# A planner for the attention part, and slot inputs by groups of four tiles, in a fused block-sparse attention and soft mixture-of-experts kernel

## The chip, the cores and the metric

The kernel runs on one core of a Trainium2 chip. The metric is the device time of one execution in microseconds. PE is the matrix engine, DVE the vector engine, ACT the scalar engine, POOL the general engine, SP the engine whose queue issues the DMAs. PE multiplies into PSUM, which has eight banks of 2 KB a partition; the other operands lie in SBUF.

## The reference

```python
# B, H, S, D = 4, 8, 768, 64; blocks of 32 rows, 24 of them
scores = scale * q @ k^T                      # scale = 1/8
mask   = |block_i - block_j| <= 1, or block_i or block_j is 0 or 23,
         or block_j is one of three sampled for block_i
attn   = softmax over the unmasked scores
x      = (attn @ v)  ->  [3072, 512]          # the eight heads side by side
# soft mixture of experts: 8 experts, 4 slots each, hidden size 1024
logits = x @ phi                              # [3072, 32]
d      = softmax(logits, over the 3072 rows)
slot_input = d^T @ x                          # [32, 512]
slot_out   = per expert: relu(slot_input @ w1) @ w2
c      = softmax(logits, over the 32 slots)
out    = c @ slot_out                         # [3072, 512], all float32
```

## The kernel before

**Attention.** Each batch has two dense query blocks (0 and 23) and 22 sparse ones, taken as 11 pairs. A pair's scores are over 256 keys for each query block: three neighbours, the two outer blocks, three sampled ones. `stage_k` puts these keys side by side in one of four buffers `kst`: POOL copies the fixed part (L214), ACT the three sampled blocks (L218), whose block numbers are loaded into registers. `stage_v` lets POOL copy the sampled V blocks into `vrs` (L229). PE multiplies queries and keys into `s` (L303) or, for the dense blocks, into `sd` (L292). DVE reduces the maximum (`nm`), ACT takes the exponential into `p`, DVE transposes it in 32 x 32 blocks into `ptt` or `ptd`, and PE multiplies with V (L375) into a product tile `avt`. `av_out` divides on DVE by the row sums and writes `x`. Eight heads are two halves `r` of four; `av_half` is one half's product for one tile. A tile `x` is 128 rows: two pairs of 64 rows, or the first pair with the dense blocks. There are six tiles in a batch.

**Slot inputs.** `moe_front` runs for each of the 24 tiles in seven steps e1 to e5: turn x (`mxt`, `xT`), logits in four parts (L487), add the parts by a product with `sel4` (L494, L495), top (`nmx`), exponential (`dT`), turn it (L517), copy `d`, sum of x weighted by d (L534), and add to `sacc` and `ssum` after scaling what was summed by `al`. Its small results lie in unused columns of `avt`.

**PSUM.** Three score banks (`SB`), two product sets of two banks, one bank for turned tiles.

**Order.** PE's and DVE's instructions stand in the order in which the loop over units writes them. `ORDER` says how dense and sparse units alternate, the lists `EOFF` after how many units each step of `moe_front` follows. Each unit is one half: a sparse unit with `r == 0` computes the scores of the whole pair. ACT, POOL and SP are ordered by the scheduler of the language.

**Weights.** 64 weight tiles of 512 KB. `NPRE` of them are loaded during attention, three into a K buffer and six into V's first buffer late in it, three more into the other K buffer; the rest comes into space that attention has released (`lwb`, V's second buffer) and into freed tiles. After attention come the experts' two layers and the combination, with the output stores.

Of the kernel before, what the change touches and what calls it, by code (L numbers as in the profile page):

```python
# [21 lines left out]
P = 128  # L22
# [13 lines left out]
NKST, NVR, NQ = 4, 6, 3  # L36
PB, PTB, XB = 4, 3, 2
SB = 3

ORDER0 = "DDSSDDSS"  # L40
ORDER = "DSSDDDSS"
KSTEP, VSTEP, EARLY = 5, 1, 4
KEARLY = 4


EOFF = [(3, 2), (5, 1), (5, 2), (6, 0), (7, 2), (7, 2), (8, 1)]
EOFFL = [(3, 1), (4, 1), (4, 2), (5, 0), (5, 1), (5, 1), (5, 2)]
# [8 lines left out]
NPRE, NLB = 12, 11  # L56
KW = {"ktile": 3, "v0": 6, "v1": 6}
W0, W1 = 3, 3
# [3 lines left out]
MAN = {mybir.EngineType.PE, mybir.EngineType.DVE}  # L62
TMAN = MAN | {mybir.EngineType.Activation}


@with_exitstack
def attn_moe_kernel(ctx, tc, qT, kT, vtab, sampled, phi, w1, w2, out):
# [49 lines left out]
    sacc = const.tile([P, P], F32, name="sacc")  # L117
# [50 lines left out]
    qd = pst.tile([P, NP, 2, BLK], F32, name="qd")  # L168
    qc = [pst.tile([P, NP, 2, BLK], F32, name=f"qc{n}") for n in range(NQ)]


    avt = psA.tile([P, 2, 2, 512], F32, name="avt", tag="av", bufs=1)
    def load_k(b):
        ktile[b] = pk.tile([P, NP, S], F32, name="ktile", tag="ktile")
        SP.dma_start(out=qd, in_=qT[b, 0])
        for p in range(NP):
            SP.dma_start(out=ktile[b][:, p, :], in_=kT[b, p])

    def load_v(b):
        vb = vbuf[b % 2].rearrange("p (a f) -> p a f", a=2)  # L180
        if b < 2:
            for p in range(NP):
                (DVE if b == 0 and p < 2 else POOL).memset(vb[32 * p:32 * p + 32, 1 - p % 2, :], 0.0)  # L183
        for p in range(NP):
            SP.dma_start(out=vb[32 * p:32 * p + 32, p % 2, :], in_=vtab[b, 32 * p:32 * p + 32, :])
        vtile[b] = vb.rearrange("p a (k r d) -> p a k r d", k=NBZ, r=2)


    def load_q(b, g):
        SP.dma_start(out=qc[(b * NG2 + g) % NQ], in_=qT[b, g + 1])  # L190

# [10 lines left out]
    def stage_k(b, i):  # L202
        n = nsp[0] % NKST
        nsp[0] += 1
        st = kst[n]
        kv = ktile[b]
        if kfresh.get(n) != b:
            kfresh[n] = b
            POOL.tensor_scalar(out=st[:, :, 128:192].rearrange("p c (g s) -> p c g s", g=2),
                               in0=kv.rearrange("p c (g s) -> p c g s", g=NB)[:, :, 0:NB:NB - 1, :],  # L210
                               scalar1=SCALE, scalar2=1.0, op0=ALU.mult, op1=ALU.mult)

        w, r0 = (0, 96) if i % 2 else (32, 0)
        POOL.tensor_scalar(out=st[:, :, w:w + 96], in0=kv[:, :, (i - 1) * BLK:(i + 2) * BLK],  # L214
                           scalar1=SCALE, scalar2=1.0, op0=ALU.mult, op1=ALU.mult)
        vals = block_numbers(sreg, i, mybir.EngineType.Activation, NB - 1)
        for j, o in enumerate((r0, 192, 224)):
            ACT.activation(out=st[:, :, o:o + BLK],  # L218
                           in_=kv[:, :, ds(vals[j] * BLK, BLK)], func=AF.Copy, scale=SCALE)
# [771 lines left out]
```

## Time and profile before

| what | value |
|---|---|
| median of 3 runs | 456.62 us (454.41 to 459.93) |
| the profiled execution | 454.29 us, its span 452.5 us, mean clock 0.885 |
| busy in the span | PE 351.7, DVE 248.1, ACT 183.9, POOL 170.5 us |
| DMA | 60.30 MB, mean 133 GB/s |

A row of a timeline is start, length, engine, line, operation, result<-operands, shape, count, and in brackets the idle time before it with what ended it. A fp32 matmul of the program is two records in the trace. A row of a stretch is its start and end, its length, busy us of PE, PEld (weight load), DVE, ACT and POOL with the number of instructions, PE's granted clock as a share of full, busy share of the DMA, and GB/s. A group's row ends in busy us, mean ns | idle time ahead of it and what ended it. A row of waits is the total in us, how often, the longest.

### The profile page before, as it was taken

Reading aid. Unit: us, or ns where it says so; the run is one execution under the profiler, and the core shown is the slowest. Engines: PE = TensorE matmul, PEld = TensorE weight load, DVE = VectorE, ACT = ScalarE, POOL = GpSimd, SP = SyncE. Lnnn points to the kernel's source line nnn. Section 1 sums busy time; section 2 is a strip of 40 time slices with the busy share of each in tenths; the row PEclk is TensorE's granted clock in tenths of the full one; section 3 lists DMA queues with packets and bytes.
Section 4 is the critical chain, followed back from the end, with each engine's and each line's share of the span. In section 5 each row is a group of like instructions: output and inputs, shape, how many; then the busy total and the mean of one; then the engine's idle time right before and its main releaser. Section 6 shows DMA issues by size and latency. Waiting matters only on the chain.

```text
span 452.5 us, 17984 instructions
## 1 busy us (share of the span) xinstructions
PE 351.7 (78%) x7381; PEld 230.7 (51%) x7381; DVE 248.1 (55%) x611; ACT 183.9 (41%) x628; POOL 170.5 (38%) x397
## 2 busy tenths in 40 slices
PE   5686977787979777878988778779786588899860
PEld 1145645454666555554855555547564356435440
DVE  7673646666556655766285558573855762401240
ACT  1544445544255545533374446252652421301340
POOL 7597145464122555633034465330433331300000
PEclk9998879899789988899698889897986887999896
DMA  8439492414310005052010043500000406999998
GB/s 237 102 114 217 169 369 91 133 47 99 76 27 28 28 13 165 27 114 63 14 38 14 25 154 116 191 25 14 26 27 1 143 1 199 403 409 406 410 335 258
DMA packets 26083, 60.30 MB, mean 133 GB/s; under 512 B 2833, under 2 KB 15250, under 8 KB 25490
## 3 DMA queue, kind: packets, MB, share of 16 engines
q1 hardware_dynamic: 26002, 59.16, 40.3%
q8 instruction: 58, 0.95, 0.9%
q14 instruction: 23, 0.19, 0.1%
HBM read 52.86 MB, written 6.29 MB: 131 GB/s over the span
## 4 chain that ended last, share of the span: by engine, by line
PE 50%; DVE 27%; DMA 11%; issue 4%; ACT 4%; ACTq 1%; DVEq 0%; SPq 0%
PE avt L375 34%; DMA w<-in_w_dram 9%; PE s L303 6%; DVE ptt L342 4%; DVE nm L319 4%; DVE x L371 4%; PE sd L292 2%; DMA kw<-in_w_dram 2%; DVE nm L310 2%; PE avt L487 2%; PE mlt L494 2%; DVE xT L329 2%; ACT p L322 2%; DVE v L183 1%; DVE rs L370 1%
## 5 line engine op out<-in xcount | busy, mean ns | idle before, releaser
L229 POOL COPY vrs<-v 128x260 f32 x264 | 96.4, 404 | 83.1 <-PE avt L375 69.7
L375 PE MATMUL avt<-v,ptt 64*64 64x130 f32 (+2 forms) x1728 | 95.2, 326 | 27.4 <-DVE sacc L539 23.1
L319 DVE TENSOR_REDUCE nm<-s 128x2 f32<-128x512 f32 x88 | 58.2, 663 | 63.2 <-PE s L303 62.9
L375 PEld LDWEIGHTS avt<-v,ptt 64*64 64x64 f32 (+2 forms) x1728 | 62.7, 150 | 55.4 <-DVE sacc L539 27.1
L218 ACT ACTIVATE kst<-ktile 128x128 f32 x264 | 63.6, 304 | 62.2 <-PE s L303 47.9
L322 ACT ACTIVATE p<-s,nm 128x256 f32<-128x256 f32 x176 | 71.9, 468 | 30.0 <-DVE nm L319 28.5
L214 POOL TENSOR_SCALAR kst<-ktile 128x384 f32<-128x384 f32 x88 | 44.1, 512 | 102.8 <-PE s L303 102.7
L303 PE MATMUL s<-kst,qc 64*32 64x256 f32 x1408 | 57.1, 400 | 6.7 <-ACT p L322 4.1
L342 DVE STREAM_TRANSPOSE ptt<-p 128x512 f32<-128x512 f32 x88 | 61.5, 698 | 0.2 <-ACT p L322 0.2
L375 PE MATMUL avt<-vrs,ptt 64*32 64x130 f32 x2112 | 56.7, 312 | 0.0
L375 PEld LDWEIGHTS avt<-vrs,ptt 64*32 64x32 f32 x2112 | 45.8, 121 | 0.4
L292 PE MATMUL sd<-ktile,qd 64*32 64x384 f32 x256 | 32.2, 584 | 16.6 <-ACT pd L316 9.8
L303 PEld LDWEIGHTS s<-kst,qc 64*32 64x32 f32 x1408 | 26.7, 110 | 23.5 <-issue 10.4
L369 DVE TENSOR_SCALAR rs<-avt 128x8 f32<-128x8 f32 (+3 forms) x33 | 5.4, 163 | 59.0 <-PE avt L375 27.0
L375 PE MATMUL avt<-v,ptd 64*64 64x130 f32 x768 | 32.4, 342 | 5.2 <-issue 3.9
L316 ACT ACTIVATE pd<-sd,nb 128x384 f32<-128x384 f32 x32 | 16.8, 576 | 45.1 <-DVE nb L313 32.6
L375 PEld LDWEIGHTS avt<-v,ptd 64*64 64x64 f32 x768 | 31.2, 177 | 6.3 <-issue 4.2
L327 ACT COPY lp<-avt 128x128 f32<-128x128 f32 x23 | 6.1, 265 | 50.1 <-issue 30.3
L292 PEld LDWEIGHTS sd<-ktile,qd 64*32 64x32 f32 x256 | 9.5, 116 | 31.9 <-ACT pd L316 14.5
L310 DVE TENSOR_REDUCE nm<-sd 128x1 f32<-128x384 f32 x32 | 16.8, 543 | 8.8 <-PE sd L292 8.5
L371 DVE TENSOR_TENSOR x<-avt,rs 128x512 f32<-128x512 f32 (+3 forms) x33 | 20.1, 609 | 1.1
L534 PE MATMUL avt<-x,d 128*32 128x128 f32 x192 | 10.8, 300 | 11.7 <-DVE d L329 11.7
(107 smaller groups left out, 354.9 us busy)
## 6 DMA issues: line engine op xcount, KB each, us to landing
w<-in_w_dram SPq DMA_DIRECT2D x34, 512.0 KB, 9.7
v<-in_w_dram SPq DMA_DIRECT2D x18, 512.0 KB, 6.3
v<-in_vtab_dram SPq DMA_DIRECT2D x16, 406.2 KB, 7.3
ktile<-in_kT_dram SPq DMA_DIRECT2D x16, 384.0 KB, 5.2
kw<-in_w_dram SPq DMA_DIRECT2D x12, 512.0 KB, 8.9
qc<-in_qT_dram SPq DMA_DIRECT2D x44, 128.0 KB, 2.1
out_dram<-ob SPq DMA_DIRECT2D x20, 256.0 KB, 4.3
qd<-in_qT_dram SPq DMA_DIRECT2D x4, 128.0 KB, 2.2
```

What stands on the lines that cost most here:

```text
L214: POOL.tensor_scalar(out=st[:, :, w:w + 96], in0=kv[:, :, (i - 1) * BLK:(i + 2) * BLK], scalar1=SCALE, scalar2=1.0, op0=ALU.mult, op1=ALU. ...
L218: ACT.activation(out=st[:, :, o:o + BLK], in_=kv[:, :, ds(vals[j] * BLK, BLK)], func=AF.Copy, scale=SCALE)
L229: POOL.tensor_copy(out=st[:, :, j:j + 1, :], in_=vf[:, :, ds(vals[j], 1), :])
L292: PE.matmul(u.s[n][32 * p:32 * p + 32, :], lhsT=qd[s_, p, u.j, :], rhs=kt[s_, p, 384 * n:384 * (n + 1)], start=True, stop=True)
L303: PE.matmul(u.pair_of[r].s[32 * p:32 * p + 32, j, :], lhsT=q[s_, p, j, :], rhs=kst_[s_, p, :], start=True, stop=True)
L310: DVE.tensor_reduce(out=nm[:, n:n + 1], in_=u.s[n], axis=AX.X, op=ALU.max, negate=True)
L316: ACT.activation(out=u.p[n], in_=u.s[n], func=AF.Exp, bias=nb, scale=SCALE)
L319: DVE.tensor_reduce(out=nm, in_=u.s, axis=AX.X, op=ALU.max, negate=True)
L322: ACT.activation(out=u.p[:, hf, :], in_=u.s[:, hf, :], func=AF.Exp, bias=nm[:, hf:hf + 1], scale=1.0)
L342: DVE.transpose(out=u.pt[:, :, n:n + 2, :].rearrange("p k j q -> p j k q"), in_=u.p.rearrange("p j (k q) -> p j k q", k=8))
L371: DVE.tensor_tensor(out=x, in0=a[:, :, :, 0:D], in1=rs[lo:hi].unsqueeze(3).to_broadcast([hi - lo, 2, 2 * n, D]), op=ALU.mult)
L375: PE.matmul(av[o:o + m, g, r * 2 * D1:(r + 1) * 2 * D1].rearrange("p (a d) -> p a d", a=2), lhsT=lhsT, rhs=rhs, start=start, stop=stop)
```

## The change

The whole of the attention and slot-input part is described as tasks with engine, estimated duration, dependencies, a key, and the buffers that they take. `Plan.run` takes the tasks one after the other, always the one that can start first by its estimates (then the one with the lower key), and so sets the order of all five engines. Some tasks may go to one of two engines.

```diff
-NKST, NVR, NQ = 4, 6, 3
-PB, PTB, XB = 4, 3, 2
-SB = 3
-ORDER0 = "DDSSDDSS"
-ORDER = "DSSDDDSS"
+NKST, NVR, NQ = 4, 6, 4
+PB, PTB, XB, XTB = 4, 4, 6, 4
+SB, MB = 4, 2
-NPRE, NLB = 12, 11
+NPRE, NLB = 7, 11
-MAN = {mybir.EngineType.PE, mybir.EngineType.DVE}
+MAN = {E_.PE, E_.DVE, E_.Activation, E_.Pool, E_.SP}
+LAG = {"PE": 0.25, "DVE": 0.18, "ACT": 0.22, "POOL": 0.17, "SP": 0.0}
+    def run(self):
...
+            for t in avail:
...
+                if ok:
+                    for e, d in t.opts:
+                        c = (max(r, at[e]), t.key, max(r, at[e]) + d)
+                        if best is None or c < best[0]:
+                            best = (c, t, e, d)
...
+            if e == "SP":
+                dma = max(dma, st + 1.4) + t.byte / 0.4e6
+                t.fin = dma + 0.3
...
+    plan = Plan(dict(s=SB, av=1, pt=MB, p=PB, ptt=PTB, kst=NKST, vrs=NVR, x=XB, xT=XTB, k=2, v=2, q=NQ,
+                     ptd=1, lp=1, dT=1, d=1), free=("pt",))
...
-    avt = psA.tile([P, 2, 2, 512], F32, name="avt", tag="av", bufs=1)
+        T.av = psA.tile([P, 2, 512], F32, name="av", tag="av", bufs=1)
...
-            for p in range(NP):
-                (DVE if b == 0 and p < 2 else POOL).memset(vb[32 * p:32 * p + 32, 1 - p % 2, :], 0.0)
+                for a in range(2):
+                    SP.dma_start(out=vb[:, a, lo:hi], in_=vfull[b, :, a * VH + lo:a * VH + hi])
...
-            POOL.tensor_scalar(out=st[:, :, w:w + 96], in0=kv[:, :, (i - 1) * BLK:(i + 2) * BLK],
-                               scalar1=SCALE, scalar2=1.0, op0=ALU.mult, op1=ALU.mult)
+            POOL.tensor_copy(out=st[:, :, w:w + 96], in_=kv[:, :, (i - 1) * BLK:(i + 2) * BLK])
...
+        r = add(sampled_, [("ACT", 0.62), ("POOL", 0.73)], [f, t_sreg], n - 2.5,
+                pre=lambda e: block_numbers(sreg, i, e, NB - 1))
...
+        t_q = add(scale, [("POOL", 0.37), ("ACT", 0.37)], [t_q], n - 4.5)
...
+        t_qk = add(qk, ("PE", 1.1), [t_q] + [k for _, k in kd], n, acq=[("s", s_use[0]), ("s", s_use[1])])
...
+            t_0 = add(lambda t: heads(t, 0), ("PE", 2.2), deps, n + 0.5, acq=[("av", use)])
+            t_a = add(lambda t: heads(t, 1), ("PE", 2.2), [t_0], n + 0.5)
+            T.out = [add(lambda t: av_out(T, T.av, 0, P), ("DVE", 1.0), [t_a], n + 0.6, acq=[("x", x_use)])]
...
+            for k in range(2):
+                for p in range(NP):
+                    for r in range(2):
+                        s_ = slice(64 * r, 64 * r + 64)
+                        PE.matmul(u.s[r][k][32 * p:32 * p + 32, :], lhsT=T.dq.q[s_, p, j, :],
+                                  rhs=kt[s_, p, 384 * k:384 * (k + 1)], start=True, stop=True)
...
+        t_qk = add(qk, ("PE", 1.5), [T.dq.t, t_k[b]], n, acq=[("s", s_use[0])] * 2 + [("s", s_use[1])] * 2)
...
+            t_a = add(dense, ("PE", 5.4), T.dturned + [t_v[b]], n + 0.5, acq=[("av", use)])
...
+    def plan_group(gi, Ts, last, final=False):
...
+            t_o = add(out, [("DVE", 0.62), ("ACT", 0.5)], [t_t], n + 2.1, acq=[("xT", x_use)])
...
+            for c in range(4):
+                for j, (_, T) in enumerate(Ts):
+                    PE.matmul(st.l[32 * j:32 * j + 32, :], lhsT=phis[:, c, :], rhs=T.xT[:, c, :],
+                              start=(c == 0), stop=(c == 3))
...
+            for j, (_, T) in enumerate(Ts):
+                PE.matmul(st.ms[32 * j:32 * j + 32, :], lhsT=st.d[:, 32 * j:32 * j + 32], rhs=T.x,
+                          start=True, stop=True)
...
+            for o, i in ((sacc, st.ms), (ssum, st.sm)):
+                if gi:
+                    DVE.scalar_tensor_tensor(out=o, in0=o, scalar=st.al, in1=i, op0=ALU.mult, op1=ALU.add)
```

In `plan_group` each of four tiles has 32 of the 128 partitions, with a top and sums of its own; `sacc` is now 128 x 512 and holds four sums, one for each place in the group. At the end the four are brought to a common top (`f_row` to `f_slots`: a turn, a small reduction, an exponential, a product with `ident`, a scaled `sel4`) and added by a product. The scale 1/8 is now applied to the queries. PSUM holds four score banks, one product set of two banks and two banks for everything else. Both halves of a dense block are multiplied together.

Where the order of instructions moves, first SP at the start of the program. `scr` is for the block numbers, `qd` and `qc` are queries of before, `q` of now, `phis` is phi. Before:

```order
L129 DMA scr<-in_sampled_dram 1x144
L609 DMA qd<-in_qT_dram 128x256
L611 DMA ktile<-in_kT_dram 128x768 x4
L190 DMA qc_105<-in_qT_dram 128x256
L185 DMA v_67<-in_vtab_dram 32x3250 x4
L190 DMA qc_106<-in_qT_dram 128x256
L615 DMA phis<-in_phi_dram 128x128
```

Now:

```order
L213 DMA scr<-in_sampled_dram 1x144
L261 DMA ktile<-in_kT_dram 128x768 x4
L272 DMA v_67<-in_vfull_dram 128x910 x6
L272 DMA v_67<-in_vfull_dram 128x520 x2
L255 DMA q<-in_qT_dram 128x256 x4
L864 DMA phis<-in_phi_dram 128x128
```

The first queries have moved behind K and V, and V is twice as large, in rows of 128 partitions.

PE between the products of two tiles in the middle of batch 1; `avt` and `av` are products, `dT`, `d` and `mxt` belong to the slot inputs. Before:

```order
L303 MATMUL s<-kst_100,qc_106 32x256 x8
L303 MATMUL s<-kst_101,qc_106 32x256 x8
L517 MATMUL avt<-ident,dT 128x32
L442 MATMUL mxt<-ident,x 128x128 x4
L534 MATMUL avt<-x,d 32x128 x4
L375 MATMUL avt<-v_68,ptt 128x130 x4
L375 MATMUL avt<-v_68,ptt 64x130 x8
```

Now:

```order
L426 MATMUL s<-kst_102,q 32x256 x8
L426 MATMUL s<-kst_103,q 32x256 x8
L426 MATMUL s<-kst_100,q 32x256 x8
L426 MATMUL s<-kst_101,q 32x256 x8
L667 MATMUL mxt<-ident,x 128x128 x4
L504 MATMUL av<-v_68,ptt 128x130 x4
L504 MATMUL av<-v_68,ptt 64x130 x8
```

Two pairs of scores and a turned tile stand there now, and the two slot-input steps that waited for other engines have gone. Before, the second of the two pairs stood between the two half products of a tile.

DVE from one tile's x on, also in batch 1. Before:

```order
L369 TENSOR_SCALAR rs<-avt 128x8
L370 RECIPROCAL rs<-rs 128x8
L371 TENSOR_TENSOR x<-avt,rs 128x512
L342 STREAM_TRANSPOSE ptt<-p 128x2x8x32
L319 TENSOR_REDUCE nm<-s 128x2
L329 COPY d<-avt 128x32
L523 SCALAR_TENSOR_TENSOR ssum<-ssum,al,sm 128x1
L329 COPY xT<-mxt 128x512
```

Now:

```order
L498 TENSOR_SCALAR rs<-av 128x8
L499 RECIPROCAL rs<-rs 128x8
L500 TENSOR_TENSOR x<-av,rs 128x512
L453 STREAM_TRANSPOSE ptt<-p 128x2x8x32 x2
L441 TENSOR_REDUCE nm<-s 128x2
L294 COPY xT<-mxt 128x512
L441 TENSOR_REDUCE nm<-s 128x2 x3
```

The slot-input steps have left the place between x and the next reductions, and a tile's two transposes stand together.

More of the change, by code (lines that the diff above doesn't have):

```diff
@@ new lines, in attn_moe_kernel, with tile_of, plan_pair, qk @@
+    tiles = {}
+    def tile_of(b, t):
+        if (b, t) not in tiles:
+            T = Rec()
+            T.b, T.t, T.turned, T.staged, T.units, T.use, T.x_use = b, t, [], [], [], [], []
+            tiles[b, t] = T
+        return tiles[b, t]
+    def plan_pair(b, g, n):
+        T = tile_of(b, (g + 1) // 2)
+        w = 1 if g and g % 2 == 0 else 0
+        u = Rec()
+        u.g = g
+        kd, ku = [], []
+        for r in range(2):
+            use = []
+            kd.append(stage_k(b, 2 * g + 1 + r, n, use))
+            ku.append(use)
+        t_q, q_use = plan_q(u, b, g + 1, n)
+        s_use = [[], []]
+        def qk(t):
+            u.s = [psA.tile([P, 2, 256], F32, tag="s", name="s", bufs=SB) for _ in range(2)]
+            for j in range(2):
@@ L360, in av_out, with new_x @@
+        u.vst = []
+        for r in range(2):
+            use = []
+            v, t_s = stage_v(b, 2 * g + 1 + r, n, use)
+            u.vst.append(v)
+            T.staged.append(t_s)
+            T.use.append(use)
+        T.units.append(u)
+        if g == 0 or w:
+            plan_av(T, n)
+    def new_x(T):
+        if not hasattr(T, "x"):
+            T.x = pw.tile([P, DM], F32, tag="x", name="x", bufs=XB)
+        return T.x
+    def av_out(T, av, lo, hi, rs_=slice(0, 2), xlo=None):
         n = rs_.stop - rs_.start
@@ new lines, in f_exp, with f_col, f_sel @@
+    def f_exp(t):
+        ACT.activation(out=fin.row, in_=fin.row, func=AF.Exp)
+    def f_col(t):
+        fin.pc = bank("mc")
+        PE.matmul(fin.pc[:, 0, 0:1], lhsT=fin.row, rhs=ident[0:1, 0:1], start=True, stop=True)
+    def f_sel(t):
+        fin.w = pw.tile([P, 1], F32, tag="w1", name="w1", bufs=1)
+        DVE.tensor_copy(out=fin.w, in_=fin.pc[:, 0, 0:1])
+        fin.sel = pw.tile([P, P], F32, tag="lp", name="selw", bufs=1)
+        DVE.tensor_scalar(out=fin.sel, in0=sel4, scalar1=fin.w, scalar2=None, op0=ALU.mult)
@@ new lines, in f_sum, with f_inv, f_slots @@
+    def f_sum(t):
+        fin.ps = bank("msum")
+        PE.matmul(fin.ps[:, 0, 0:1], lhsT=fin.sel, rhs=ssum, start=True, stop=True)
+    def f_inv(t):
+        fin.tot = pw.tile([P, 1], F32, tag="tot", name="tot", bufs=1)
+        DVE.tensor_scalar(out=fin.tot, in0=fin.ps[:, 0, 0:1], scalar1=EPS, scalar2=None, op0=ALU.add)
+        DVE.reciprocal(out=fin.tot, in_=fin.tot)
+    def f_slots(t):
+        fin.sS = bank("psS")
+        for c in range(4):
+            PE.matmul(fin.sS[:, c, 0:NS], lhsT=sacc[:, c * P:(c + 1) * P], rhs=fin.sel[:, 0:NS], start=True, stop=True)
@@ L695, in attn_moe_kernel @@
[L695 to L707 removed]
+    plan.run()
     ms.__exit__(None, None, None)
@@ L711, in attn_moe_kernel @@
     ms.__enter__()
[L712 to L750 removed]
+    ssum = fin.tot
     att.close()
```

968 lines of the change are left out of this document (533 added, 435 removed).

## The prediction

> **What bounds the kernel now.** I read the totals of the page first, then its slices, to see which stages there are.
>
> ```profile
> span 452.5 us, 17984 instructions
> PE 351.7 (78%) x7381; PEld 230.7 (51%) x7381; DVE 248.1 (55%) x611; ACT 183.9 (41%) x628; POOL 170.5 (38%) x397
> ...
> PE   5686977787979777878988778779786588899860
> ...
> PEclk9998879899789988899698889897986887999896
> DMA  8439492414310005052010043500000406999998
> ```
>
> No engine is full. One slice is 11.3 us: attention reaches to about slice 33 (PE at seven or eight tenths, DMA mostly idle), then come seven slices with the DMA full. They need separate sums. Next the chain and PE's waits:
>
> ```profile
> PE 50%; DVE 27%; DMA 11%; issue 4%; ACT 4%; ACTq 1%; DVEq 0%; SPq 0%
> ...
> PE avt L375 <- DVE sacc L539: 23.1, 12, 2.8
> PE avt L534 <- DVE d L329: 11.7, 16, 2.0
> ```
>
> The chain alternates between PE and DVE, and PE's two longest waits are for `sacc` and `d`, both of the per-tile slot-input chain. One tile, PE and then DVE, shows how:
>
> ```profile
> 239.45 2.93 PE L375 MATMUL avt<-v,ptt 64*128 64x130 f32 x40 [1.81 <-DVE sacc L539]
> ...
> 243.18 0.43 PE L487 MATMUL avt<-xT,phis 128*32 128x128 f32 x8
> 243.54 1.09 PE L303 MATMUL s<-kst,qc 64*32 64x256 f32 x32
> 244.56 0.49 PE L494 MATMUL mlt<-lp,sel 128*128 128x128 f32 x2
> ...
> 245.12 1.71 PE L375 MATMUL avt<-v,ptt 64*128 64x130 f32 x40
> ...
> 247.45 1.09 PE L303 MATMUL s<-kst,qc 64*32 64x256 f32 x31
> 249.04 0.21 PE L517 MATMUL avt<-ident,dT 32*128 32x32 f32 x1 [0.50 <-ACT kst L218]
> 249.19 0.66 PE L442 MATMUL mxt<-ident,x 128*128 128x128 f32 x4
> ...
> 252.49 0.38 PE L375 MATMUL avt<-v,ptt 64*128 64x130 f32 x2 [1.82 <-DVE sacc L539]
> ...
> 244.72 0.69 DVE L319 TENSOR_REDUCE nm<-s 128x2 f32<-128x512 f32 x1 [4.71 <-PE s L303]
> ...
> 248.21 0.69 DVE L371 TENSOR_TENSOR x<-avt,rs 128x512 f32<-128x512 f32 x1
> ...
> 252.11 0.32 DVE L539 SCALAR_TENSOR_TENSOR sacc<-sacc,al,avt 128x128 f32<-128x128 f32 x1
> ```
>
> DVE waits 4.71 us for scores while PE multiplies; later DVE works without a pause and PE waits for it. They take turns, and a tile takes 13.04 us from product to product. The stretches:
>
> ```profile
> 213.50:302.00 88.50, 72.18 (x1718) 51.27 (x1718) 53.15 (x129) 41.59 (x148) 35.96 (x92) 0.88 0.22 73
> 239.45:252.49 13.04, 10.32 (x266) 7.44 (x266) 7.46 (x18) 6.73 (x26) 5.92 (x17) 0.88 0.08 23
> 151.67:163.38 11.71, 8.94 (x266) 6.32 (x266) 7.52 (x18) 6.73 (x26) 6.61 (x17) 1.00 0.09 25
> 372.00:374.00 2.00, 2.00 (x30) 1.43 (x33) 1.64 (x6) 0.00 (x0) 1.77 (x6) 0.56 0.10 16
> ```
>
> The columns are the stretch, then busy time of PE, PEld, DVE, ACT and POOL, the clock, and DMA. A batch takes 88.50 us, of which PE is idle 16.3. The same tile at clock 1.00 takes 11.71 us: PE's pauses cost 1.3 us more through the lower clock that follows them. The first half product of the tile above took 3.73 us (239.45 to 243.18), the second, without a pause, 2.33 (245.12 to 247.45).
>
> **The change, PE's work.** The planner's PE order is known, so I price it at full-clock pitches, start to start. Further rows:
>
> ```profile
> 206.10 1.49 PE L292 MATMUL sd<-ktile,qd 64*32 64x384 f32 x16
> 207.53 1.34 PE L375 MATMUL avt<-v,ptt 64*64 64x130 f32 x18
> ...
> 209.58 0.43 PE L487 MATMUL avt<-xT,phis 128*32 128x128 f32 x8
> ...
> 36.02 3.11 PE L375 MATMUL avt<-v,ptd 64*64 64x130 f32 x99 [0.40 <-DVE x L371]
> 43.06 5.25 PE L375 MATMUL avt<-v,ptd 64*64 64x130 f32 x93 [3.94 <-issue]
> ```
>
> - 44 score pairs at 1.02 us (243.54 to 244.56): 44.9.
> - 8 dense score blocks, now both row halves interleaved. A pair, interleaved already, takes 1.02 us for 32 x 256 columns; by that rate 32 x 384 take 1.53: 12.2. Bounds: 1.43 each (the second half wholly beside the first, 206.10 to 207.53) and 2.86 (no overlap), so 11.4 to 22.9. I take 12.2, the nearer kind of row. Today it is 16 x 1.43 = 22.9.
> - 40 half products at 2.33: 93.2. Four first-pair products with both halves interleaved: one half takes 2.05 (207.53 to 209.58), so between 2.05 and 4.1; I take 2.4 since the halves use different columns of the array: 9.6.
> - 4 dense products: 99 of 192 records took 3.11, so 6.0 each: 24.0.
> - 24 turned tiles at 0.66: 15.8. Logits and sums: the columns stay the same, four rounds of 0.43 per group of four tiles, 12 x 1.7 = 20.6. Twelve small transposes at 0.21: 2.5. The products with `sel4` (0.56 a tile) are gone.
>
> Sum: 222.8 us of PE work, 55.7 a batch, against 72.2 busy now.
>
> **The change, the other engines.** Per tile DVE loses `d`, `ssum`, `sacc`, the top and mostly `xT` (the order puts 20 of 24 on ACT). What stays is eight instructions of at most 0.69 us and x with two short steps, 6.6 of the 7.46 at most. ACT gives up 27 of 88 sampled K copies and three quarters of the small copies and takes xT: I leave it at its 6.73. POOL takes those 27 and 20 of the 48 query scalings, the order says. Two rows, the one of `vrs` with least, median and largest ns:
>
> ```profile
> L229 POOL COPY vrs<-v x264: 394/403/535, 28.0 to 372.5; 128x260 f32 x132
> ...
> L322 ACT ACTIVATE p<-s,nm 128x256 f32<-128x256 f32 x176 | 71.9, 468 | 30.0 <-DVE nm L319 28.5 <-DVE d L329 0.7 <-DVE rs L369 0.2
> ```
>
> At 0.4 us or less an instruction that adds about 1.5 us a tile to the 5.92 to 6.61 of now: some 7.7. PE's tile is 2 x 2.33 + 2 x 1.02 + 0.66 + a quarter group (1.0) = 8.4. So PE becomes the longest, POOL stands close behind.
>
> What stays as PE's pauses. With one product set the next tile's product waits until DVE has written x: in the tile above that is at 248.90, 1.45 us after PE went on to the next scores (247.45). Two score pairs and a turn stand between the products in the new order, 2.7 us of work: that is the cover. It holds only while the four score banks are free in time, that is while eight exponentials (0.47 us mean or less) end within the 4.7 us of two half products. I leave 0.6 us a tile for what slips (12), 4 us a batch in the dense part, where one block takes all four banks and the next scores must wait for its exponentials (16), and 4 for fetch pauses such as the 3.94 us above. 32 in all; bounds 12 (half the tile's slip, nothing else) and 75 (today's 16.3 a batch plus lost clock). With it a batch takes 63.7 us.
>
> **The start.** V of batches 0 and 1 now comes with its zeros, 3.33 MB instead of 1.66 with memsets, and the queries stand behind it in SP's queue.
>
> ```profile
> 5.36 3.53 PE L292 MATMUL sd<-ktile,qd 64*32 64x384 f32 x6 [5.36 <-DMA ktile<-in_kT_dram]
> ...
> 4.00:8.00 4.00, 2.64 (x5) 0.53 (x6) 3.24 (x3) 0.00 (x0) 2.98 (x2) 1.00 1.04 381
> 12.00:16.00 4.00, 1.21 (x2) 0.00 (x0) 2.08 (x6) 1.40 (x7) 3.96 (x4) 1.00 0.97 199
> ...
> 7.37 0.35 SPq L615 DMA_DIRECT2D phis<-in_phi_dram  x1
> ...
> phis<-in_phi_dram SPq DMA_DIRECT2D x1, 64.0 KB, 10.9
> ```
>
> K rows over 128 partitions moved at 381 GB/s, V rows over 32 partitions at 199. `phis`, issued behind V at 7.37, landed 10.9 us later, with V: what stands behind V waits for it. The new V spans 128 partitions, so 1.57 + 3.33 + 0.13 MB at 381 from 3 us on: 16.2, with the scaling 17.5 us until the first scores (5.36 today). At 199 for V it would be 25. I take 17.5 because width decides between the two rows.
>
> **The end.** From the last product on the DMA sets the pace.
>
> ```profile
> 380.48 1.67 PE L375 MATMUL avt<-vrs,ptt 64*32 64x130 f32 x46
> ...
> 372.00:382.15 10.15, 8.75 (x189) 6.57 (x189) 2.93 (x12) 0.98 (x5) 2.58 (x7) 0.68 0.51 168
> 390.00:400.00 10.00, 9.54 (x84) 3.60 (x84) 2.08 (x10) 1.84 (x4) 3.20 (x6) 1.00 1.03 410
> ...
> w<-in_w_dram SPq DMA_DIRECT2D x34, 512.0 KB, 9.7
> ```
>
> The last product ends at 382.15, 70.35 us before the end. `NPRE` falls from 12 to 7: five tiles of 512 KB (0.524 MB) more in this stage, 6.4 us at 410 GB/s. Today the last tile's two half products lie apart, and from 372.00 to 382.15 the DMA already moved 168 GB/s x 10.15 us = 1.7 MB of weights. With both halves together at the end some of that falls behind them, between 0 and 4.1 us; I take 3, nearer to the upper end since the order lets V's space go only with the last product. 79.8. The new merge of the four sums (seven small steps) lies beside the weight stream.
>
> **Sum**: 17.5 + 222.8 + 32 + 79.8 = 352 us of span. The profiled execution took 454.29 with a span of 452.5, so add 1.8: **354 us**. That execution lies 0.5% under the median of 456.62 (runs from 454.41 to 459.93), and I forecast on its scale.
>
> [...] The slow products stand behind pauses of 1.81 and 1.82 us. [...]
>
> **The rivals.**
> - *The single product set becomes the turn-taking.* If the score banks come free late, nothing covers the 1.4 us and the next half product runs at 3.73 instead of 2.33. 20 tiles x 2.8 = 56 instead of 12, and 2 us more in each dense part: 354 + 44 + 8 = **406**. For it: every tile shows this pair of costs today. Against it: the order runs scores a tile ahead.
> - *Nearly gapless*: only 12 us lost, **334**. Against it: DVE and POOL have little slack.
> - *POOL held up by DVE*: if POOL stands still while DVE transposes, four instructions of x's size (0.69) a tile add 2.8 to 7.7 and POOL's 10.5 us replace 9.0: 20 x 1.5 = 30 more, **384**. Against it: `vrs` has a median of 403 ns beside a least of 394, and no copy took over 535. [...]
> - *Slower: the clock.* A fixed order on all five engines may spread short pauses evenly, so that PE stays at the clock of 372 to 374, 0.56. At 3.73/2.33 = 1.6 times, the work takes 356: 17.5 + 356 + 32 + 79.8 + 1.8 = **487**. It turns slower than before once three quarters of the work (100 of the 134 us extra) run so. Against it: the mean is 0.88 with longer pauses than I expect.
> - *It does not act*: queue positions of loads eat the gain. A batch's K and V take 12.9 us at 381 GB/s, while four query buffers cover about four pairs; only with new stalls of some 25 us a batch would it end level, near **456**.
>
> **How the numbers follow.** Forecast, 328 to 380: 0.64; gapless below 328: 0.06; product set 0.18; POOL 0.04; unchanged 0.03; clock 0.05. The range 328 to 402 holds the forecast, POOL's case and rather more than half of the product set's. 1% is about what a measurement of this kernel can tell from no change. Faster by over 1%: 0.64 + 0.06 + 0.18 + 0.04 = 0.92; within 1%: 0.03; slower: 0.05.
>
> **What would show it.** First scores near 17.5 us; the last product near 272; tiles of 8.5 to 9.5 us with the second half product right behind the first and clock near 1.00; DVE busy near 6 us a tile of about 9; a DMA-full stage of about 80 us with 45 weight tiles in it. I am wrong in PE's sum if batches take 64 us with PE idle in them much above 8, in the cover if PE waits for x or for exponentials at every tile, in the end if the weight stream is not what ends last.

## The result, and the profile after

The changed kernel takes **365.61 us** (median of 4 runs, 363.07 to 369.46) against 458.04 us (4 runs, 454.41 to 459.93) for the kernel before: a ratio of 0.797, 95% interval 0.789 to 0.805. Predicted were 354 us with a range of 328 to 402. The profiled execution of after is the longest of its four (369.46 us, clock 0.933 against 0.946 to 0.952 in the others), so the sizes below are also read from a second profile of the same kernel, `base`, whose execution took 365.78 us. Times are medians of all runs and ratios are of the fast runs; between fast runs alone the differences below move by up to 2 us.

The page of after: span, busy totals, the slices of PE, its clock and the DMA, and the chain.

```profile
span 367.5 us, 17242 instructions
PE 288.2 (78%) x7113; PEld 188.6 (51%) x7113; DVE 215.7 (59%) x494; ACT 166.9 (45%) x511; POOL 179.0 (49%) x498
...
PE   0078888999679799878898589799978569998740
...
PEclk9999999999899969999999899899978867999985
...
DMA  7902960220296003007817206610222998999997
...
PE 56%; DMA 14%; DVE 12%; issue 7%; ACT 4%; SPq 2%; ACTq 1%; POOL 0%; DVEq 0%
```

A slice is now 9.2 us. The first two are loads alone, attention fills slices 3 to 31, the DMA-full end the rest. In the chain DVE fell from 27% to 12%. The longest waits of PE (total, times, longest):

```profile
PE sd L593 <- DMA phis<-in_phi_dram: 17.7, 1, 17.7
PE av L504 <- issue: 8.6, 8, 1.9
PE s L426 <- issue: 7.3, 3, 3.9
PE s L426 <- ACT pd L612: 7.2, 4, 2.6
PE mxt L667 <- DVE x L500: 4.9, 6, 1.3
...
PE avd L504 <- issue: 1.5, 1, 1.5
```

Of the waits for `sacc` and `d` that headed this list before (23.1 and 11.7 us), that for `sacc` is gone and that for `d` is down to 1.1 us. In their place stand pauses whose releaser is "issue": PE waited for nothing that the profile shows. One tile on PE, its last product, and the stretches of the tile and of all attention:

```profile
186.70 1.71 PE L504 MATMUL av<-v,ptt 64*128 64x130 f32 x40
...
189.06 1.71 PE L504 MATMUL av<-v,ptt 64*128 64x130 f32 x40
...
193.34 0.66 PE L667 MATMUL mxt<-ident,x 128*128 128x128 f32 x4 [0.59 <-DVE x L500]
...
194.95 1.71 PE L504 MATMUL av<-v,ptt 64*128 64x130 f32 x40
...
287.50 0.42 PE L504 MATMUL av<-vrs,ptt 64*32 64x130 f32 x6 [1.55 <-issue]
```

```profile
186.70:194.95 8.25, 7.66 (x245) 5.41 (x244) 6.11 (x12) 6.54 (x21) 8.25 (x25) 1.00 0.25 61
...
17.70:287.96 270.26, 232.87 (x6574) 161.01 (x6574) 192.52 (x412) 146.02 (x457) 166.20 (x466) 0.96 0.36 111
```

This tile, without a fetch pause, takes 8.25 us at full clock, against 13.04 before (11.71 there at full clock), and its second half product follows 2.36 us after the first (186.70 to 189.06). Attention ends at 287.96; the end takes 367.5 - 287.96 = 79.5 us. Of the 85 us between the two profiled spans, attention gives 106.5 (270.26 against 376.79 us from first score to last product); a start 12.3 us later and an end 9.2 us longer take 21.5 back. With the profile of `base` it is 111.2 (its stretch is shown below), and 22.5 taken back.

### The profile page after: what moved, and what is told of

Same layout as the page of the kernel before. It is cut to its first block, busy times and chain, and to the rows that moved or that the text cites. A ratio compares the mean times of both kernels' runs of the same rounds, so it can differ in the third digit from the quotient of the medians.

```text
span 367.5 us, 17242 instructions
## 1 busy us (share of the span) xinstructions
PE 288.2 (78%) x7113; PEld 188.6 (51%) x7113; DVE 215.7 (59%) x494; ACT 166.9 (45%) x511; POOL 179.0 (49%) x498
## 4 chain that ended last, share of the span: by engine, by line
PE 56%; DMA 14%; DVE 12%; issue 7%; ACT 4%; SPq 2%; ACTq 1%; POOL 0%; DVEq 0%
PE av L504 24%; PE s L426 11%; PE avd L504 6%; DMA w<-in_w_dram 6%; PE mxt L667 3%; DMA v<-in_w_dram 3%; PE sd L593 3%; DMA q<-in_qT_dram 3%; PE pf L1029 2%; DVE x L500 2%; DMA v<-in_vfull_dram 2%; PE ms L735 2%; DVE ptd L616 2%; PE ml L685 2%; ACT p L446 1%
## 5 line engine op out<-in xcount | busy, mean ns | idle before, releaser
L504 PE MATMUL av<-v,ptt 64*64 64x130 f32 (+2 forms) x1728 | 78.0, 293 | 3.7 <-issue 2.8
L446 ACT ACTIVATE p<-s,nm 128x256 f32<-128x256 f32 x176 | 72.0, 477 | 17.4 <-DVE nm L441 15.8
L504 PEld LDWEIGHTS av<-v,ptt 64*64 64x64 f32 (+2 forms) x1728 | 52.4, 136 | 33.5 <-issue 23.7
L453 DVE STREAM_TRANSPOSE ptt<-p 128x512 f32<-128x512 f32 x88 | 58.4, 692 | 18.5 <-ACT p L446 18.3
L426 PE MATMUL s<-kst,q 64*32 64x256 f32 x1408 | 57.5, 417 | 14.6 <-issue 7.3
L347 POOL COPY kst<-ktile 128x384 f32<-128x384 f32 x88 | 43.3, 508 | 35.9 <-PE s L426 32.7
L504 PE MATMUL av<-vrs,ptt 64*32 64x130 f32 x2112 | 47.2, 281 | 5.8 <-issue 5.8
L353 ACT ACTIVATE kst<-ktile 128x128 f32 x183 | 42.3, 303 | 20.2 <-PE s L426 18.6
L426 PEld LDWEIGHTS s<-kst,q 64*32 64x32 f32 x1408 | 32.2, 113 | 30.4 <-issue 21.1
L504 PEld LDWEIGHTS av<-vrs,ptt 64*32 64x32 f32 x2112 | 36.6, 107 | 7.8 <-issue 7.7
L292 ACT COPY xT<-mxt 128x512 f32<-128x512 f32 x21 | 12.2, 583 | 47.5 <-PE mxt L667 47.5
L605 DVE TENSOR_REDUCE nm<-sd 128x1 f32<-128x384 f32 x32 | 16.6, 548 | 18.2 <-PE sd L593 18.0
L504 PE MATMUL avd<-v,ptd 64*64 64x130 f32 x768 | 23.2, 272 | 2.7 <-issue 1.5
L504 PEld LDWEIGHTS avd<-v,ptd 64*64 64x64 f32 x768 | 21.8, 133 | 5.2 <-issue 2.2
```

Source lines behind the costliest of these rows:

```text
L347: POOL.tensor_copy(out=st[:, :, w:w + 96], in_=kv[:, :, (i - 1) * BLK:(i + 2) * BLK])
L353: ACT.activation(out=st[:, :, o:o + BLK], in_=src, func=AF.Copy, scale=1.0)
L426: PE.matmul(u.s[r][32 * p:32 * p + 32, j, :], lhsT=u.q[s_, p, j, :], rhs=kd[j][0][s_, p, :], start=True, stop=True)
L446: ACT.activation(out=u.p[r][:, j, :], in_=u.s[r][:, j, :], func=AF.Exp, bias=u.nm[r][:, j:j + 1], scale=1.0)
L453: DVE.transpose(out=T.pt[r][:, :, 2 * w:2 * w + 2, :].rearrange("p k j q -> p j k q"), in_=u.p[r].rearrange("p j (k q) -> p j k q", k=8))
L504: PE.matmul(av[o:o + m, g, r * 2 * D1:(r + 1) * 2 * D1].rearrange("p (a d) -> p a d", a=2), lhsT=lhsT, rhs=rhs, start=start, stop=stop)
```

## The experiments

Every time is a median; a ratio is to the kernel before in the same set of runs, with its 95% interval.

### base: the changed kernel again

> The changed kernel as it is, for its time on this chip beside the others of this set, and for a second profile of it. Expected 363 to 368 us, first scores at 17.7 us, and the pauses of TensorE with no releaser ("issue") at 12 to 18 us again, in the same stretches with 200 GB/s and more, if they belong to the program; a few us and elsewhere, if they were an accident of the one profiled execution.

364.18 us, ratio 0.792 (0.786 to 0.799). Its attention stretch and its pauses without a releaser, in that stretch:

```profile
17.70:283.29 265.59, 226.98 (x6574) 155.62 (x6574) 193.98 (x412) 146.21 (x458) 166.12 (x467) 0.98 0.36 113
...
PE av L504 <- issue: 11.2, 9, 3.0
...
PE s L426 <- issue: 3.8, 3, 1.7
...
PE avd L504 <- issue: 1.6, 1, 1.6
```

16.6 us of such pauses, after 17.4 in the first profile: they belong to the program. PE is idle 38.6 us of 265.6, of which 0.3 lie ahead of the first scores (18.02).

### qfirst: queries ahead of V

```diff
-        t_q = add(load, ("SP", 0.45), [], n - 6, acq=[("q", use)], byte=131072)
+        t_q = add(load, ("SP", 0.45), [], n - 6 if n > 1 else -17 + 0.1 * n, acq=[("q", use)], byte=131072)
```

> The queries of the first two items are issued between the first batch's K and its V, instead of behind V. Theory (the start is the time in which K, V and queries arrive one behind the other): the first scores start at 8 to 10 us instead of 17.7, as the 3.1 MB of V no longer stand ahead of them; the first products still want V at about 17 us, so 4 to 8 us of the 8 to 9 come back in the total (357 to 361 us). Rival (queries and V share the queues, so that the order of issue says little): first scores still at 15 us or later, and no gain that can be told from the changed kernel.

356.29 us, ratio 0.781 (0.776 to 0.786). First scores and first product:

```profile
9.63 2.82 PE L593 MATMUL sd<-ktile,q 64*32 64x384 f32 x32 [9.63 <-ACT q L388]
...
20.99 2.38 PE L504 MATMUL av<-v,ptt 64*64 64x130 f32 x36
```

The scores start 8.4 us earlier than in `base` (18.02), the first product 7.3 us earlier (28.31 there), and 7.9 us arrive in the total, the upper end of the 4 to 8 expected. The order in one queue decides, as the prediction's start term assumed, and 8 us of that term were avoidable.

### paced: K and V in pieces

Each later batch's four K and four V pieces become tasks of their own, each one depending on the scores of a later item.

```diff
-        t_k[b] = add(lambda t: load_k(b), ("SP", 1.9), go, first[b] - 20 if b else -20,
...
+        for p in range(NP):
+            dep = [qks[first[b] - 8 + p // 2], t_k[b]]
+            t_k[b] = add(lambda t, p=p: load_k(b, p), ("SP", 0.48), dep, first[b] - 20,
...
+        for c in range(4):
+            dep = [qks[first[b] - 6 + c], t_v[b]]
+            t_v[b] = add(lambda t, c=c: load_v(b, c), ("SP", 1.0 if b < 2 else 1.9), dep, first[b] - 16,
```

> K and V of the second, third and fourth batch are issued in eight pieces over successive items, instead of in one burst each. Theory (TensorE's pauses without a releaser are its instruction fetch, which stands behind the bulk load in the DMA queues): these pauses fall from 17 us to 8 us or less, the granted clock behind them rises, and the time falls by 6 to 12 us (354 to 360 us). Rival (the pauses have another cause, such as the program's own order): they stay at 14 us or more and the time within 1% of the changed kernel. Second rival: the loads come too late for the batch and the pauses turn into waits of the first scores of a batch for K, with the time up by 3 us or more.

359.30 us, ratio 0.783 (0.776 to 0.790). The interval still overlaps that of `base`. PE's waits:

```profile
PE s L438 <- issue: 6.7, 5, 2.8
PE av L516 <- issue: 6.4, 6, 2.3
```

13.1 us of pauses instead of 16.6, not 8: spreading the pieces shortens the pauses, it does not remove them. The time is 4.9 us lower, not 6 to 12. The direction is the theory's, the size is not, and by this run alone the rival (14 us or more, time within 1%) is not far off.

### noload: later K and V not loaded

```diff
     def load_k(b):
+        if b:
+            ktile[b] = ktile[0]
+            return
...
     def load_v(b):
+        if b:
+            vtile[b] = vtile[0]
+            return
```

> K and V of the second to fourth batch are not loaded (all batches compute with the first one's; that part of the work is left out); the order of all instructions is unchanged. Theory (TensorE's pauses without a releaser are its own instruction packets queued behind these bulk loads): of the 16.6 us of such pauses only those behind the weight loads are left, 3 to 6 us; with the clock behind them the time falls by 10 to 16 us, to 348 to 355 us. Rival (the pauses belong to the instruction stream itself, one at each refill of so many instructions): 12 us or more of them stay, and the time falls by less than 4 us.

355.77 us, ratio 0.777 (0.773 to 0.782). PE's waits:

```profile
PE av L510 <- DMA v<-in_w_dram: 8.6, 1, 8.6
...
PE s L432 <- issue: 5.2, 4, 2.4
...
PE av L510 <- issue: 1.5, 1, 1.5
```

Of 16.6 us of pauses 6.7 remain, just above the theory's 3 to 6, and the rival's 12 or more is excluded. The edit brought a wait of its own, 8.6 us: the fourth batch now reads the first V buffer, into which weights are already loaded. The time is 8.4 us lower in spite of it, short of the theory's 10 to 16; how much more it would be without that wait was not tried. So most of these pauses come with the bulk loads. The three longest that remain (1.54, 1.72 and 2.42 us) follow weight loads issued at most 12 us ahead.

The edit moved weights as well: V's second buffer is never used here, and six weight tiles go into it at 15.65 us, ahead of all of attention. The end moves less for it (last column GB/s, 349 in `base`) and is hardly shorter than the 80.5 us of `base`:

```profile
275.00:354.60 79.60, 54.61 (x543) 27.40 (x539) 20.71 (x65) 16.08 (x37) 8.00 (x16) 0.88 0.83 304
```

### npre2: two weight tiles loaded ahead

```diff
-NPRE, NLB = 7, 11
+NPRE, NLB = 2, 11
```

> Two weight tiles instead of seven are loaded ahead of the end, so that 50 instead of 45 are streamed in it. Theory (the end is bound by the weight stream, so that the change from 12 to 7 cost five tiles of 1.28 us): the end grows by 6.4 us and the total by 5 to 7 us. Rival (the wait ahead of the first expert's products, now that they start 16.7 us behind the last product of attention, hides those tiles): total within 2 us of the changed kernel.

377.68 us, ratio 0.827 (0.822 to 0.832), 13.5 us slower than `base`. In the profiles the end grows from 363.8 - 283.29 = 80.5 us to 371.1 - 279.88 = 91.2: 10.7 us for five tiles, 2.1 each instead of the 1.28 that I priced. Both the theory's 5 to 7 us and the rival's 2 were too low. The profiled execution, 372.99 us, is the shortest of its five, so the 10.7 comes from one pair of profiles. Two stretches of the end of `npre2` say in part why (last column GB/s):

```profile
296.80:306.80 10.00, 9.98 (x72) 2.87 (x76) 0.00 (x0) 0.59 (x1) 0.00 (x0) 0.77 0.81 273
...
336.80:346.80 10.00, 5.91 (x64) 2.86 (x56) 2.38 (x4) 3.18 (x6) 0.00 (x0) 0.95 0.89 283
```

The stream runs at 407 to 410 GB/s only in some stretches of the end. It drops to 273 and 283 in these (306 and 334 in the two such stretches of `base`), and there the DMA queue waits for the experts' products, up to 7.8 us at a time, before it can load into their tiles. With `noload`, whose end has six tiles less to stream and lasts as long, this says that the end is not set by the bytes of the stream alone. PE's mean clock in the end is lower as well, 0.79 against 0.84 in `base`; how much of the 10.7 us is clock was not told apart.

### dense_apart: a dense block's halves as two tasks

```diff
-        t_qk = add(qk, ("PE", 1.5), [T.dq.t, t_k[b]], n, acq=[("s", s_use[0])] * 2 + [("s", s_use[1])] * 2)
+        t_qk0 = add(lambda t: qk(t, 0), ("PE", 1.4), [T.dq.t, t_k[b]], n, acq=[("s", s_use[0])] * 2)
+        t_qk = add(lambda t: qk(t, 1), ("PE", 1.4), [T.dq.t, t_k[b], t_qk0], n, acq=[("s", s_use[1])] * 2)
```

> The scores of a dense block's two halves are issued as two tasks of 16 products again, each half on its own two banks and 64 rows of the array, and not as one task of 32 that alternates between the halves. Theory (four products of different rows and columns stand side by side only in the joint form, as in the prediction's 1.53 against 2.86 us a block): TensorE's busy time grows by 8 to 11 us, the total by 6 to 11 us, to 370 to 375 us. Rival (the dense part is bound by its softmax, since TensorE waits there for it four times by 1.9 to 2.6 us in any case): busy time up, but the total within 3 us of the changed kernel.

360.79 us, ratio 0.792 (0.784 to 0.800): the ratio of `base`. A joint block of `base`, and one half in `dense_apart`:

```profile
82.09 1.54 PE L593 MATMUL sd<-ktile,q 64*32 64x384 f32 x32
```

```profile
79.96 1.49 PE L594 MATMUL sd<-ktile,q 64*32 64x384 f32 x16
```

My price per undisturbed block, 1.53 against 2 x 1.43, is near what the rows show. The dense scores' busy time is 26.5 us against 18.3; even the joint form is above the 12.2 of my sum, since some blocks run at half clock (2.82 us for the first, at 18.02) or are split by a wait. The total does not see the difference: PE's idle time in attention is 29.5 us here (the row of `dense_apart` below), 38.6 in `base`. So the theory's 370 to 375 us is wrong and the rival's forecast near. Its reason, that the softmax bounds the dense part, is not shown: the waits for `pd` fall from 7.2 to 5.3 us, the rest of the difference is spread over many waits, and the edit also lets a half's maximum start ahead of the other half's scores.

### sb3, mb1 and banks_old: what the PSUM split is worth

```diff
-SB, MB = 4, 2
+SB, MB = 3, 2
```

All three start from `dense_apart`. The diff is that of `sb3`; `mb1` has `SB, MB = 4, 1`, and `banks_old` has `SB, MB = 3, 1` with two product sets (`av=2`).

> The eight PSUM banks split as in the kernel before (three for scores, two product sets of two banks each, one for transposes) and the dense halves' scores apart, under the changed order and the inputs by four tiles. Theory (one product set with back-to-back halves costs nothing, and four score banks let the scores run ahead): this is dense_apart and some more, as the third bank stops the second score pair and one bank of transposes blocks the sums' chains: 372 to 390 us. Rival (the single product set makes the halves take turns, the prediction's first rival): the second set gives time back, and this runs within 2 us of dense_apart or under it.

> dense_apart with three score banks instead of four; one product set and two transpose banks stay, and one PSUM bank is left unused. It tells which bank of the old split costs its 58 us (banks_old 418.6 against dense_apart 360.8). Theory (a score pair takes two banks, so with three the second pair's second half waits until the first pair's softmax has read its banks, as the waits of the scores for ScalarE's p and pd, 32.5 us in banks_old against 5.3 in dense_apart, say): 395 to 415 us. Rival (the transpose bank was it, for the sums' chain and the transposes of x share it): within 8 us of dense_apart, 357 to 368 us.

> dense_apart with one transpose bank instead of two; four score banks and one product set stay, one PSUM bank is left unused. Theory (score banks carry the gain): 3 to 15 us slower than dense_apart, 364 to 376 us, by waits at the transposes of x, the logits and the sums. Rival (the transpose bank carries it): 395 us or more.

| kernel | score banks | product sets | transpose banks | us | ratio |
|---|---|---|---|---|---|
| dense_apart | 4 | 1 | 2 | 360.79 | 0.792 (0.784 to 0.800) |
| mb1 | 4 | 1 | 1 | 370.07 | 0.809 (0.804 to 0.813) |
| sb3 | 3 | 1 | 2 | 413.92 | 0.905 (0.902 to 0.909) |
| banks_old | 3 | 2 | 1 | 418.58 | 0.915 (0.907 to 0.924) |

By the medians the fourth score bank carries 53 us, the second transpose bank 9 (by the ratios 52 and 8, since the rows come from two sets of runs). `sb3` and `mb1` lie in the ranges expected of them; `banks_old` is 29 us above its own. With three score banks, a second product set in place of the second transpose bank brings nothing (419 against 414); if a transpose bank is worth 9 there too, the second set is worth some 5 at most, an estimate from these rows. Four score banks with two product sets were not tried; with a transpose bank they would need nine banks. Attention's stretch in `dense_apart`, then in `sb3` with its waits for ScalarE:

```profile
17.80:278.42 260.62, 231.13 (x6574) 160.74 (x6574) 192.48 (x413) 143.20 (x447) 168.39 (x475) 0.99 0.37 115
```

```profile
17.60:329.15 311.55, 256.27 (x6574) 166.72 (x6574) 193.90 (x410) 144.67 (x438) 172.29 (x487) 0.91 0.31 96
...
PE s L426 <- ACT p L446: 15.8, 10, 3.1
PE s L426 <- ACT pd L616: 12.8, 7, 2.3
...
213.15 0.62 PE L426 MATMUL s<-kst,q 64*32 64x256 f32 x2
215.00 1.09 PE L426 MATMUL s<-kst,q 64*32 64x256 f32 x30 [1.24 <-ACT p L446]
```

The last two rows show the mechanism. A pair takes two banks, one for each half, and its products alternate between them. With three banks the pair starts, stops after two records on the bank that is still unread, and waits 1.24 us for the exponential ahead of the tile's product. Of the 50.9 us that attention grows, 25.8 are idle time (55.3 against 29.5) and 25.1 are busy time. By the ratio of the mean clocks (0.91 here, 0.99 there) some 20 of these are the clock, an estimate, so the waits cost nearly as much again through it.

### keyorder: the lowest key instead of the earliest start

```diff
+        self.late = self.opts[0][0] == "PE" and abs(key - round(key)) > 0.45
...
-                        c = (max(r, at[e]), t.key, max(r, at[e]) + d)
+                        c = (t.key + (1.5 if t.late else 0.0), max(r, at[e]), max(r, at[e]) + d)
```

> The planner takes the allowed task of the lowest key instead of the one that can start earliest (products, whose key lies half an item ahead, are put 1.5 items behind so that the scores still run ahead), with all buffers, banks and arithmetic the same. Theory (what the order is worth is the filling of a wait on one engine with whatever is ready; in the kernel before a tile lost 4.4 us to such waits): TensorE's idle time between first score and last product grows by 40 to 100 us, the time is 400 to 460 us. Rival (the dependencies alone set the pace, so that any list in order of the items runs alike): within 10 us of the changed kernel.

432.29 us, ratio 0.951 (0.941 to 0.961):

```profile
17.70:343.49 325.79, 244.85 (x6574) 156.35 (x6574) 194.16 (x410) 133.03 (x399) 189.36 (x547) 0.92 0.28 90
...
PE mxt L668 <- DVE x L501: 27.8, 25, 1.3
...
PE md L727 <- ACT dT L720: 11.7, 6, 3.6
```

PE's idle time is 80.9 us instead of 38.6, and busy time grows by 17.9 at a clock of 0.92. The waits for x and for the steps of the slot inputs return, at every tile and every group. With the same banks and the same arithmetic the rule of the earliest start is worth 68 us against this one other rule.

### one_tile: slot inputs after every tile

```diff
-    for gi in range(6):
-        Ts = done[4 * gi:4 * gi + 4]
+    for gi in range(24):
+        Ts = done[gi:gi + 1]
```

Each step of the group then works on 32 partitions.

> The slot inputs are taken up after every tile, on 32 partitions, in 24 groups of one instead of 6 of four, under the same planner. Theory (the chain of a tile costs 1.7 us of TensorE, some 2.5 us of VectorE and 1.5 us of ScalarE whatever its width, and TensorE waits little for it, since the planner puts other work into it): TensorE's busy time up by 25 to 35 us and the total by 25 to 40 us, to 390 to 405 us. Rival (the order hides it, because TensorE has room in its pauses): total up by less than 10 us. Second rival (the chain itself was what the grouping took off the path, as in the kernel before): up by 60 us or more.

396.88 us, ratio 0.868 (0.859 to 0.878); its stretch, and the groups of logits and sums (busy, mean ns | idle before), then those of `base`:

```profile
18.30:315.47 297.17, 261.49 (x6627) 171.88 (x6628) 224.14 (x493) 158.42 (x513) 171.94 (x488) 0.97 0.32 99
...
L737 PE MATMUL ms<-x,d 128*32 128x512 f32 x48 | 27.5, 658 | 3.6 <-DVE d L296 3.3
L687 PE MATMUL ml<-xT,phis 128*32 128x128 f32 x192 | 25.5, 275 | 4.4 <-DVE xT L296 2.4 <-issue 1.9
```

```profile
L685 PE MATMUL ml<-xT,phis 128*32 128x128 f32 x192 | 7.8, 294 | 0.3 <-ACT xT L292 0.3
L735 PE MATMUL ms<-x,d 128*32 128x512 f32 x48 | 6.6, 626 | 1.1 <-DVE d L294 1.1
```

PE's busy time grows by 34.5 us, its idle time does not (35.7 against 38.6). The size is the theory's, and the rows say more than it did: the same 192 and 48 records take 53.0 us one tile at a time and 14.4 four at a time, while a single record takes as long (658 and 275 ns against 626 and 294). So those of a group run beside each other; in the kernel each of the four tiles writes 32 partitions of its own.

### best: three edits of the order together

`qfirst`, `paced`, and the last group's turn moved from ahead of the first expert into the experts' loop:

```diff
+        if g == 5:
+            z = add(lambda t: c_head(5), ("DVE", 0.55), [c, t_7], k + 1.25, acq=[("p", [t_7])])
+            add(lambda t: c_rest(5), ("POOL", 0.95), [z], k + 1.3)
+            continue
...
+        if n == 4:
+            c_turn(5, c4[5], psF.tile([P, 4, P], F32, tag="po", name="pc", bufs=3))
```

> Three edits of schedule together: the first two items' queries between K and V (qfirst, -8 us), K and V of the later batches in pieces (paced, -5 us), and the last turned group's transposes moved from ahead of the first expert into the experts' loop. Theory: the first two add up, as one shortens the start and the other the pauses behind it, and the third lets the first expert start 3 to 4 us earlier; since the end is bound by its weight stream, it is worth 0 to 3 us: 346 to 352 us. Rival (the weight stream starts when attention ends and does not care when the first expert starts): 350 to 353 us with an end of 80 us as before. Second rival (the later V pieces collide with the last items): no better than qfirst, 355 us or more.

351.79 us, ratio 0.769 (0.765 to 0.772): below both kernels, and below `qfirst` and `base` with intervals that do not touch. So the start and the loads add up, as far as the third edit brought nothing; its share was not measured alone. It did not do what it says:

```profile
284.53 1.12 PE L855 MATMUL pc<-ident,c 128*128 128x128 f32 x4 [3.71 <-DVE cm L807]
...
286.32 5.35 PE L1045 MATMUL pf<-w,sT 128*32 128x512 f32 x24 [0.68 <-ACT cT L295]
```

Another turn stands in the same place, with a longer wait (3.71 us for `cm` instead of 2.83 for `c`). The first expert starts 17.4 us after the last product (268.93), 16.6 in `base`, and the end takes 80.8 us, which is what the rival said (80 as before).

## Why the prediction was right, and where it was off

**Right in sign, in mechanism and within its range**, 11.6 us too low. Of the sum, against `base`:

| term | predicted | measured | how |
|---|---|---|---|
| start | 17.5 | 18.0 | to the first scores |
| PE's work | 222.8 | 227.0 | busy, at a mean clock of 0.98 |
| fetch pauses | 4 | 16.6 | three "issue" rows |
| other pauses | 28 | 21.7 | 38.3 - 16.6 |
| end | 79.8 | 80.5 | 363.8 - 283.29 |

**Where the gain comes from.** Attention is 111 us shorter than before (376.8 to 265.6): 37 us of PE's idle time (76.0 to 38.6) and 74 of its busy time (300.8 to 227.0). By the clock changes in the two traces about 102 us of the busy time before and 16 now lie at half clock; the time ahead of the first change is counted with it, since the joint dense block at 18.02 in `base` takes 2.82 us and the one at 82.09 takes 1.54. So some 43 us of the gain are clock and some 31 work that is no longer there, an estimate. A wait that is gone counted twice here: as a wait, and through the clock behind it.

**The step that was mis-sized is "4 for fetch pauses".** I had taken one row of 3.94 us from the trace of before as all there would be; 16.6 us come. The term is sized by the runs; that it has to do with the bulk loads is shown by `noload` (6.7 us left) and, weaker, by `paced` (13.1). No row names a releaser of these pauses, but the trace does say what PE waits for. PE's instructions come in packets of 16 KB in a queue of their own (queue, packets, MB, share of the DMA engines' time, for all of `base`):

```profile
q8 instruction: 56, 0.92, 1.1%
```

That is one packet for some 254 of the 7113 matmul and 7113 weight-load records. Of the 13 pauses of `base`, 12 end 1.2 to 1.7 us after such a packet has landed, and the records at which they stand are multiples of 256 apart, to within one (behind record 962, 1217, 1473, 4290, 4545, 5057, 7617, 8898, 9410, 12481, 12738, 13250). All five pauses of `noload` do the same, and so do 11 of the 12 of after. So these pauses are refills of PE's instructions that come late; the thirteenth, 1.34 us behind record 6782, has another cause. Each stands at a refill, as the rival of `noload` said, but only some refills are late, and most of those come with the bulk loads, as the theory said. In `base` 23 of 56 refills begin within 1.75 us of their packet's landing, in the kernel before 4 of 58, so more refills are late now; they were not hidden in other waits. What makes the packets late inside the machine stays open.

**The start** came out as priced with the width of V's rows as the argument (the DMA moved 372 GB/s from 3 to 16 us of `base`), and `qfirst` confirms its cause, the order in the queue. The width alone was not varied.

**The pauses of tile and dense part** were put too high, by 6 us: 0.6 us a tile and 4 a batch. PE waits four times for `pd`, 7.2 us in all, and for x at five tiles, 4.4. A batch takes 66.3 us on average, with PE idle for 9.6 of them, where I had 63.7 and 8. The cover that I named, scores running a tile ahead while four score banks are free in time, is the condition on which much of the gain rests: `sb3` takes one bank away and lands 53 us higher, at 414, near the 406 of the first rival. That rival had the condition right, late score banks, and the cost wrong. In `sb3` PE waits for the exponentials (15.8 and 12.8 us in the rows above) and little for x, and `banks_old` has two product sets and is no faster. That the times are near each other is luck.

**The end's** sum was right and its split was not. Five tiles cost 6.4 by the stream's rate and 10.7 by `npre2`, so the DMA's rate alone does not set the pace there; I had added 3 for an overlap that is lost. At 2.1 us a tile no such term is needed to get from 70.35 to 80.5. Which it is in the step from 12 to 7 was not tried.

**PE's work** was right where it could be read from rows of the same kind (joint dense block 1.54 against 1.53, half product 2.36 against 2.33), and 4.2 us short in sum. This is in part luck, as two errors of opposite sign meet in it. The 16 us at half clock add some 8 us, so at full clock the price was some 4 us too high (estimates as above). And the logits and sums, priced at 20.6 as if four tiles stood one after the other, take 14.4 (rows under `one_tile`). The joint dense scores, where I counted 10.7 us saved, are worth nothing in time (`dense_apart`).

**The other rivals.** POOL is not held up: the row of `vrs` in after, with least, median and largest ns, reads

```profile
L371 POOL COPY vrs<-v x264: 399/404/537, 17.2 to 280.7; 128x260 f32 x132
```

against 394/403/535 before, beside a DVE that is busier per microsecond (192.5 of the 270.3 us of attention, 226.1 of 376.8 before). The clock did not fall (0.96 to 0.98 in attention, 0.88 before). Nearly gapless, 334 us, it is not either: 38.3 us of idle time are left, not 12.

Taken apart, the order is worth 68 us (`keyorder`), the fourth score bank 53, the groups of four 33. Together that is 154 for a gain of 92, as it would be if they need each other: the order can run ahead only into free banks. No run takes two of them away at once, so this stays a reading.

## What to carry to other kernels

Before an order is improved, count the buffers that let one engine run ahead: here one PSUM bank, taken from a double buffer, was worth 53 us, the planner's rule 68. Price a wait together with the clock behind it, which nearly doubled its cost in `sb3`. When PE becomes nearly gapless, look at the "issue" pauses, at when PE's instruction packets land and at what the DMA does just ahead of them; a queue order that puts small urgent loads first, and bulk loads in pieces, gave another 12 us here (in `best`).

## What the runs showed of the hardware that was not expected

The length of a pause alone does not say whether the clock falls. In `base` PE stood still from 205.87 to 208.91 us, 3.04 us, and the clock stayed at 1.00; it stood still from 228.38 to 230.94, 2.55 us, and the clock fell. The clock's changes in the trace of `base`, from the first up to the end of attention, stand at 26.63, 94.90, 98.31, 129.03, 132.45, 231.43 and 234.85 us: all are whole multiples of 3.413 us apart. The two pauses by the stretches of that grid (PE's busy time behind the length, clock in the third column from the end), and then the pause of 3.91 us in after, by its own grid:

```profile
204.13:207.54 3.41, 1.74 (x73) 1.25 (x71) 2.37 (x4) 1.61 (x5) 3.05 (x8) 1.00 0.50 184
207.54:210.95 3.41, 2.04 (x52) 1.52 (x52) 0.49 (x2) 1.58 (x7) 1.65 (x7) 1.00 0.03 7
...
228.02:231.43 3.41, 0.86 (x19) 0.16 (x6) 3.31 (x9) 1.07 (x3) 0.72 (x3) 1.00 1.03 387
231.43:234.85 3.42, 3.42 (x63) 1.67 (x62) 3.04 (x6) 2.21 (x6) 1.64 (x4) 0.50 0.33 124
```

```profile
202.51:205.93 3.42, 0.00 (x0) 0.00 (x0) 1.21 (x3) 0.00 (x0) 3.34 (x11) 1.00 0.28 107
205.93:209.34 3.41, 3.32 (x47) 2.30 (x48) 1.74 (x3) 0.00 (x0) 1.97 (x5) 0.50 0.14 43
```

The longer pause of `base` is split between two stretches that are 49% and 40% idle, the shorter one falls into one stretch that is 75% idle, and the clock is halved in the stretch behind that. In the attention of `base` the three stretches with 72% to 75% idle are followed by half clock, and no stretch with 50% or less is; in after one with 51% is. So in these traces PE's idle share within a fixed stretch tells more than the length of a pause, and several short pauses in one stretch add up: the stretch ahead of the slow product at 239.45 in the kernel before, 235.71 to 239.12, is 64% idle. A sharp limit does not come out of the runs: in the kernel before a stretch with 31% idle (184.51 to 187.92) is followed by half clock, in `paced` one with 52% (261.26 to 264.67) is not, so what PE does in its busy time may count as well. Also, the DMA moved only 29 GB/s from 205.90 to 208.90 us: the pause outlasts the bulk load that it follows, and its instruction packet starts only at 206.47 us.
